# Loads of the first value tiles through GpSimd's queue, masks handed to VectorE later, and a key copy one head sooner, in a fused attention and mixture-of-experts kernel

## The chip, the cores and the metric

The kernel runs on one core of a Trainium2 chip. The metric is the time of one execution in device microseconds (us); lower is better. The core has five engines with a queue each: PE (TensorE, matmuls; its weight loads are listed apart as PEld), DVE (VectorE), ACT (ScalarE), POOL (GpSimd) and SP (SyncE, here used for DMA alone). DMA transfers are started by SP, ACT and POOL and carried out by 16 DMA engines which all of them share. The profile names lines of the kernel as L12.

## The reference

Inputs are q, k and v (4 batches, 8 heads, 768 positions, 64 values a head), the router's probabilities (3,072 rows by 4 experts), and w1 (4 x 512 x 1024) and w2 (4 x 1024 x 512), all float32. Attention is causal; heads 0, 2 and 6 ("retrieval") see all earlier positions, the other five ("streaming") the first 4 positions and the last 64. Its output, 3,072 rows of 512, goes through four experts whose outputs are added with normalised probabilities:

```python
scores = scale * np.matmul(q, k.transpose(0, 1, 3, 2))
causal = rel >= 0
stream_keep = causal & ((pos[None, :] < 4) | ((rel >= 0) & (rel < 64)))
mask = np.where(retr, causal, stream_keep)
a = softmax(np.where(mask, scores, -1e9))       # per row, + 1e-9 in the sum
x = (a @ v).transpose(0, 2, 1, 3).reshape(3072, 512)
p = probs / (probs.sum(-1, keepdims=True) + 1e-9)
for e in range(4):
    out += p[:, e:e + 1] * (np.maximum(x @ w1[e], 0.0) @ w2[e])
```

## The kernel before

**Tiles and stages.** The 3,072 rows are 24 tiles of 128. The first four tiles are the first 128 positions of the four batches. They need only the keys and values of the same 128 positions, so they are computed in a stage of their own at the start ("first" functions, L969 to L1106). The other 20 tiles get their attention in eight groups: group g is batch g // 2 and half g % 2 of its positions (384 each; half 0 leaves out the first 128). Their experts run in ten pairs of tiles.

**The start.** For each first tile b, `turn_first` transposes q and k with TensorE, `scores_first` makes scores and their exponentials (for tiles 2 and 3 `mask_scores_first` multiplies a mask afterwards; for tiles 0 and 1 the mask is a bias that `masks_first` puts into PSUM first), `values_first` multiplies with the values in `v_first`, `turn_back_first` transposes the result into `x_first`, and `layer1_first` multiplies with w1 of expert 0. w1 is in two halves of 512 columns; `layer1_first(b, [0])` needs half 0, `layer1_first(b, [1])` half 1. When all four tiles are there, `layer2_first` multiplies with w2 of expert 0. The order of these calls is written out in L1555 to L1592 and is the order of TensorE's queue.

**Loads of the start.** q and k of tiles 0 and 1 go out first, k from SP and q from ACT (L394 to L397). `load_first_v` loads the values of tile 0 from ACT and those of tiles 1 to 3 from SP as float32 into parts of the tile hA, and `cast_first_v` has VectorE turn them into float16 in `v_first` (a part of the tile tsb): L376 to L383. GpSimd's queue takes the loads that change float32 into float16 on the way: w1(0) half 0, the rows of q and k of tiles 2 and 3 (`load_first_rows`), w1(0) half 1, w2(0), and then the other weights and the inputs of attention (L483 to L502). Each load of w1's halves is two DMAs; `load_first_rows` is four.

**The other stages.** `moe_steps` yields pieces of the experts' work: first experts 1 to 3 on the four first tiles (`plain_steps`, L950), then the ten pairs (`pair_steps`, L1209), for which layers 1 and 2 are done in part by a scheme of seven products in place of eight, whose sums of blocks are VectorE's work (L843). Between these pieces the loop at the end (L1639) puts steps of attention. When, is set by `plan`: for each group a begin and an end in units of "spent" time, which counts every step by its planned length times a share (0.8 and 1.2 for the first tiles' experts, 0.5 for layer 1 of a pair and PSHARE = 1.57 for layer 2). While a group is behind its plan, one attention step after another is put in. `scale_inputs` calls `require`, which puts in whatever of a group is still missing when a pair needs it.

**A group of attention** (L512). `keys_to_rows` (L248) copies keys of retrieval heads from kT into kR with VectorE in two parts; part 0 stands at the group's beginning. Then for each head in the order 0, 2, 6, 1, 3, 5, 7, 4: `scores` multiplies into a bank of PSUM (L578), ScalarE takes the exponential into `es` (L587), and VectorE multiplies the mask into it (L594 or L598) right behind. `values` comes some heads later (a list `waiting`): TensorE multiplies `es` with the values into one of two PSUM buffers pV (L628 for retrieval, L682 for streaming heads). A retrieval head's buffer is freed by VectorE's L655 to L659, a streaming head's by ScalarE's L697 and L706 and then VectorE's L702. L702 is not put into VectorE's queue at once: `later` keeps it until the planned clock has gone on by LAG = 1,300 ns. The next group's keys and queries are transposed by DMA from SP (`transpose_k`, `transpose_q`) after the fourth head of group 1 and the third of later groups.

Engines work their queues in order, so an instruction that waits holds what stands behind it on its engine.

Of the kernel before, what the change touches and what calls it, by code (L numbers as in the profile page):

```python
# [11 lines left out]
FP32 = mybir.dt.float32  # L12
# [7 lines left out]
def kernel(  # L20
# [355 lines left out]
    def load_first_v(eng, b):  # L376
        n0 = (0, 2 * H * D, 4 * HT * 4 * P, 4 * HT * 4 * P + 2 * H * D)[b]
        x = hA[:, n0 : n0 + 2 * H * D].bitcast(FP32)
        vf[b] = x.rearrange("p (h d) -> p h d", h=H)
        eng.dma_start(out=vf[b], in_=v[b, :, 0:P, :].rearrange("h p d -> p h d"))  # L380

    def cast_first_v(b):
        nc.vector.tensor_copy(out=v_first[:, b, :, 0:D], in_=vf[b])  # L383

    vf = {}
# [12 lines left out]
    load_first_v(nc.scalar, 0)  # L398
    load_first_v(nc.sync, 1)
# [11 lines left out]
    for b in (2, 3):  # L411
        load_first_v(nc.sync, b)
# [69 lines left out]

    load_w1(0, 0)  # L483
    load_first_rows(2)
    load_first_rows(3)
    load_w1(0, 1)
# [25 lines left out]
    def attention(b, c):  # L512
# [57 lines left out]
        pv_of = {}  # L570
        def scores(h):
            hp = h // 2
            es_of[h] = []
            for cols, parts, masks in score_tiles(h):
# [15 lines left out]
                for m, mo, o0, o1 in masks:  # L590
                    if m is mC:
                        x = es[:, o0:o1].rearrange("p (n x) -> p n x", x=P)
                        y = mC.rearrange("p (n x) -> p n x", n=1)
                        nc.vector.tensor_tensor(  # L594
                            out=x, in0=x, in1=y.to_broadcast(list(x.shape)), op=ALU.mult
                        )
                        continue
                    nc.vector.tensor_tensor(  # L598
                        out=es[:, o0:o1],
                        in0=es[:, o0:o1],  # L600
                        in1=m[:, mo : mo + o1 - o0],
                        op=ALU.mult,
                    )
# [66 lines left out]
        def values(h):  # L670
            if RETR[h]:
                yield from values_r(h)
                return
# [63 lines left out]
        keys_to_rows(b, c, 0)  # L737
# [26 lines left out]
        for h in waiting:  # L764
            yield from values(h)
            behind_values(h)
        if g == 0:
            transpose_k(*more)
            transpose_q(*more)
# [49 lines left out]
    def later(op, g):  # L819
        behind.append((clock[0] + LAG, op, g))  # L820
# [388 lines left out]
    def pair_steps(nt0, nxt):  # L1209

        def plain_layer1(e):
            xs = scaled(e)
            for f0 in range(0, FTP, 2):
# [19 lines left out]
                yield 2 * DMP * mm_ns(PC), 0.5  # L1233
# [5 lines left out]
        def winograd_layer1(e, x, y, kept=kept):  # L1239
# [37 lines left out]
            yield ns, 0.5  # L1277
# [407 lines left out]
```

## Time and profile before

| what | value |
|---|---|
| median of 3 runs (lowest to highest) | 387.23 us (387.05 to 387.24) |
| the profiled execution, its own time | 387.16 us |
| its span in the trace | 385.5 us |
| PE busy from 0 to 34.91 us | 24.23 us |
| PE busy from 34.91 to 42 us | 7.09 us |
| PE busy from 42 to 380 us | 331.76 us |
| PE busy from 380 to 385.5 us | 2.27 us |
| packets in GpSimd's DMA queue, whole span | 95,872, 19.81 MB |

The span is the time from the first to the last instruction of the profiled execution; the remaining 1.66 us of that execution lie around it. "Idle before" in a row is the time for which an engine stood still ahead of that instruction, and the name behind the arrow is what it waited for by the semaphores.

### The profile page before, as it was taken

The numbers are of one execution on the slowest core, as the hardware profiler recorded it, in microseconds if no ns is written. First come the engines' busy times: TensorE is split into PE (matmuls) and PEld (weight loads), VectorE is DVE, ScalarE is ACT, GpSimd is POOL, SyncE is SP. The second block draws the span as 40 slices with busy tenths as digits, with TensorE's granted clock in tenths as the row PEclk, the third lists the DMA queues.
The fourth block names the chain that finished last, engine by engine and source line by source line (L and its number), as shares of the span: only waits on it lengthen the run. The fifth ranks groups of instructions, "written<-read, shape, count | busy, mean of one in ns | idle before, by whom it ended". The sixth has DMA issues, their size and how long they took to land.

```text
span 385.5 us, 10312 instructions
## 1 busy us (share of the span) xinstructions
PE 365.4 (95%) x4223; PEld 308.0 (80%) x4223; DVE 271.1 (70%) x614; ACT 226.5 (59%) x450; POOL 123.9 (32%) x163
## 2 busy tenths in 40 slices
PE   7489999899979999999999999899999999999996
PEld 4366445448878987998898999798898899998996
DVE  4272762977678867568857867976767967989882
ACT  2164368644876785775785695685687262360630
POOL 7526758463028338058173184220000000000000
PEclk9799999999999999999999999999999999999999
DMA  7999999999149999589599499592111110300101
GB/s 171 201 207 210 127 189 176 170 130 214 58 76 130 101 122 164 108 116 119 85 150 124 80 148 115 72 176 30 37 41 57 52 60 0 111 3 0 58 2 56
DMA packets 134376, 40.93 MB, mean 106 GB/s; under 512 B 119976, under 2 KB 128776, under 8 KB 134328
## 3 DMA queue, kind: packets, MB, share of 16 engines
q0 software_dynamic: 95872, 19.81, 62.0%
q1 hardware_dynamic: 36264, 18.62, 21.6%
q10 hardware_dynamic: 2192, 1.84, 1.5%
q8 instruction: 33, 0.54, 0.6%
q14 instruction: 15, 0.12, 0.1%
HBM read 47.00 MB, written 6.34 MB: 138 GB/s over the span
## 4 chain that ended last, share of the span: by engine, by line
PE 83%; DVE 7%; DMA 5%; ACT 3%; issue 1%; DVEq 0%; ACTq 0%
PE pO L1399 26%; PE pA L1217 22%; PE pO L1246 9%; PE pO L926 6%; PE pA L956 5%; PE pA L578 4%; DMA hA<-in_v_dram 3%; PE pV L1246 2%; PE pA L1246 2%; PE pA L1091 2%; PE pV L628 2%; PE pV L682 2%; DMA xT<-x_one 1%; DVE xs L1168 1%; DVE kS L269 1%
## 5 line engine op out<-in xcount | busy, mean ns | idle before, releaser
L1399 PEld LDWEIGHTS <-hA 128*128 128x128 f16 x1104 | 105.5, 98 | 12.2
L1217 PE MATMUL pA<-xs,w1sb 128*128 128x256 f16 x768 | 96.9, 272 | 0.0
L1399 PE MATMUL pO<-w2sb,hA 128*128 128x256 f16 x640 | 77.5, 272 | 0.0
L1217 PEld LDWEIGHTS <-w1sb 128*128 128x128 f16 x768 | 71.5, 98 | 7.4
L1226 ACT ACTIVATE hA<-pA 128x512 f16<-128x512 f32 x96 | 57.0, 600 | 31.5 <-PE pA L1217 20.2
L587 ACT ACTIVATE es<-pA 128x384 f16<-128x384 f32 (+2 forms) x112 | 52.4, 497 | 23.4 <-PE pA L578 15.3
L285 POOL DMA_DIRECT2D vS<-in_v_dram x40 | 37.1, 941 | 83.8 <-PE pV L682 62.3
L1399 PE MATMUL pO<-tsb,hA 128*128 128x256 f16 x464 | 56.2, 272 | 0.0
L1168 DVE TENSOR_TENSOR xs<-xT,pB 128x512 f16<-128x512 f16 (+1 forms) x53 | 47.2, 915 | 1.5 <-DMA qT<-q 1.5
L843 DVE TENSOR_TENSOR hA<-hA 128x1024 f16<-128x1024 f16 x60 | 39.5, 684 | 0.5
L1246 PEld LDWEIGHTS <-w1sb 128*128 128x128 f16 x512 | 31.2, 98 | 1.2 <-issue 0.5
L702 DVE TENSOR_TENSOR xT<-pV,rc 64x256 f16<-64x256 f32 (+1 forms) x40 | 19.5, 488 | 15.3 <-ACT rc L706 12.3
L1419 ACT COPY s<-pO 128x256 f32<-128x256 f32 x31 | 11.5, 372 | 31.2 <-PE pO L1399 25.4
L926 PE MATMUL pO<-w2sb,hA 128*128 128x512 f16 x128 | 29.5, 379 | 0.0
L210 POOL DMA_DIRECT2D k_rows<-in_k_dram x24 | 21.5, 906 | 12.9 <-DMA kT<-k_rows 12.9
L1256 ACT COPY s<-pO 128x512 f32<-128x512 f32 x39 | 22.7, 589 | 3.4 <-PE pO L1246 2.9
L697 ACT ACTIVATE rc<-pV,eps 64x256 f32<-64x256 f32 (+1 forms) x40 | 20.9, 522 | 5.5 <-PE pV L682 4.8
L1263 DVE CUSTOM_DVE_ANT_0 hA<-pO,s 128x512 f16<-128x512 f32 x26 | 17.7, 687 | 8.9 <-PE pO L1246 4.5
L598 DVE TENSOR_TENSOR es<-es,mW 128x256 f16<-128x256 f16 (+1 forms) x40 | 12.3, 318 | 14.7 <-ACT es L587 14.6
L926 PEld LDWEIGHTS <-hA 128*128 128x128 f16 x128 | 12.1, 98 | 12.9
L578 PE MATMUL pA<-qT,kR 128*128 128x128 f16 (+2 forms) x132 | 21.1, 263 | 1.0 <-DVE kR L251 1.0
L956 PE MATMUL pA<-x_first,w1sb 128*128 128x512 f16 x96 | 21.8, 379 | 0.0
(163 smaller groups left out, 536.3 us busy)
## 6 DMA issues: line engine op xcount, KB each, us to landing
pB<-p_rows SPq DMA_DIRECT2D x10, 512.0 KB, 5.1
out_dram<-o SPq DMA_DIRECT2D x19, 256.0 KB, 3.2
w1sb<-in_moe_w_dram POOLq DMA_DIRECT2D x16, 256.0 KB, 11.7
w2sb<-in_moe_w_dram POOLq DMA_DIRECT2D x4, 1024.0 KB, 13.5
k_rows<-in_k_dram POOLq DMA_DIRECT2D x24, 128.0 KB, 5.4
q<-in_q_dram POOLq DMA_DIRECT2D x20, 128.0 KB, 6.8
vS<-in_v_dram POOLq DMA_DIRECT2D x20, 112.0 KB, 5.7
vS<-in_v_dram POOLq DMA_DIRECT2D x20, 80.0 KB, 5.5
```

What stands on the lines that cost most here:

```text
L285: gp.dma_start(out=t[:, t0(c) :, own_v(h)], in_=windows_of(v, b, h, c))
L578: nc.tensor.matmul(out=ps[:, o : o + nq], lhsT=key_tile(b, c, h, t), rhs=qTs[b, c][:, hp, q0 : q0 + nq], start=True, stop=True,)
L587: nc.scalar.activation(out=es[:, 0:cols], in_=ps[:, 0:cols], func=AF.Exp, scale=SC)
L843: nc.vector.tensor_tensor(out=out, in0=a, in1=b, op=ALU.subtract)
L926: nc.tensor.matmul(out=ps_o, lhsT=hs[:, ft, nt * P : (nt + 1) * P], rhs=w2sb[:, e * FTP + ft, :], start=(ft == 0), stop=(ft == FTP - 1),)
L956: nc.tensor.matmul(out=ps, lhsT=w1_tile(e, ct, ft), rhs=x_first[:, ct, :], start=(ct == 0), stop=(ct == DMP - 1),)
L1168: nc.vector.tensor_tensor(out=o, in0=xin, in1=pb.to_broadcast([P, DMP, n, P]), op=ALU.mult)
L1217: nc.tensor.matmul(out=ps[:, f * PC : (f + 1) * PC], lhsT=w1_tile(e, ct, f0 + f), rhs=xs[:, ct, :], start=(ct == 0), stop=(ct == DMP - 1),)
L1226: nc.scalar.activation(out=blocks[:, b0 : b0 + 2, k0 : k0 + 2, :].rearrange("p t f x -> p f t x"), in_=ps.rearrange("p (f t x) -> p f t x" ...
L1246: nc.tensor.matmul(out=ps[:, f * P : (f + 1) * P], lhsT=w_tile(e, w[:, ct, :], f), rhs=a[:, ct, :], start=(first and f == 0 and ct == 0), ...
L1256: nc.scalar.copy(out=kept[n], in_=ps)
L1399: nc.tensor.matmul(out=ps, lhsT=a[:, k, :], rhs=b(k), start=(first and k == 0), stop=(k == KT - 1), skip_group_check=not first,)
```

## The change

- The values of the four first tiles are loaded by GpSimd, which changes them into float16 on the way, straight into `v_first`; the four casts are gone. In GpSimd's queue v of tile 0 stands first, v of tile 1 behind w1(0) half 0, v of tiles 2 and 3 ahead of w2(0).
- w1(0) half 1 stands between the rows of tiles 2 and 3, and no longer behind both.
- TensorE's order of the first tiles is changed from tile 2 on: layer 1 of tile 0, half 1, and of tile 1, half 0, come ahead of tile 3's transposes; the values of tile 2 ahead of tile 3's scores.
- Masks are handed to VectorE by `later` with a lag of 800 ns of the planned clock behind the scores; `values` hands over what is left of its head's. The list `behind` is kept in order of due time.
- For groups from 2 on, part 0 of `keys_to_rows` stands in the group before, behind the first of the heads that are left in `waiting`.
- The plan: the shares of the first pair are 0.8 and 1.24, those of the others as they were; attention 1 may begin at the first pair's beginning, and the ends of groups 1 to 7 are later.

The diff, cut:

```diff
-    def load_first_v(eng, b):
-        n0 = (0, 2 * H * D, 4 * HT * 4 * P, 4 * HT * 4 * P + 2 * H * D)[b]
-        x = hA[:, n0 : n0 + 2 * H * D].bitcast(FP32)
-        vf[b] = x.rearrange("p (h d) -> p h d", h=H)
-        eng.dma_start(out=vf[b], in_=v[b, :, 0:P, :].rearrange("h p d -> p h d"))
-
-    def cast_first_v(b):
-        nc.vector.tensor_copy(out=v_first[:, b, :, 0:D], in_=vf[b])
+    def load_first_v(b):
+        gp.dma_start(
+            out=v_first[:, b, :, 0:D], in_=v[b, :, 0:P, :].rearrange("h p d -> p h d")
+        )
...
-    load_first_v(nc.scalar, 0)
-    load_first_v(nc.sync, 1)
...
-    for b in (2, 3):
-        load_first_v(nc.sync, b)
...
+    load_first_v(0)
     load_w1(0, 0)
+    load_first_v(1)
     load_first_rows(2)
+    load_w1(0, 1)
     load_first_rows(3)
-    load_w1(0, 1)
+    load_first_v(2)
+    load_first_v(3)
     load_w2(0)
...
+        def mask_later(es, masks):
+
+            left = [masks]
+
+            def run():
+                for m, mo, o0, o1 in left.pop() if left else ():
...
+            later(run, g, MASK_LAG)
+            return run
...
-                for m, mo, o0, o1 in masks:
...
+                masks_of.setdefault(h, []).append(mask_later(es, masks))
...
         def values(h):
+            for run in masks_of[h]:
+                run()
...
-        keys_to_rows(b, c, 0)
+        if g < 2:
+            keys_to_rows(b, c, 0)
...
-        for h in waiting:
+        for n, h in enumerate(waiting):
             yield from values(h)
             behind_values(h)
+            if more and g and n == 0:
+                keys_to_rows(*more, 0)
...
+    MASK_LAG = 800.0
+
-    def later(op, g):
-        behind.append((clock[0] + LAG, op, g))
+    def later(op, g, lag=LAG):
+        behind.append((clock[0] + lag, op, g))
+        behind.sort(key=lambda x: x[0])
...
+        share1, share2 = (0.8, 1.24) if nt0 == pair0 else (0.5, PSHARE)
...
-    cast_first_v(0)
     scores_first(0)
     turn_first(1, [0])
     values_first(0)
-    cast_first_v(1)
...
     turn_first(2)
-    cast_first_v(2)
     turn_back_first(1)
-    turn_first(3)
     scores_first(2)
     mask_scores_first(2)
-    cast_first_v(3)
+    layer1_first(0, [1])
     layer1_first(1, [0])
+    turn_first(3)
+    values_first(2)
     scores_first(3)
-    values_first(2)
     mask_scores_first(3)
-    layer1_first(0, [1])
+    layer1_first(1, [1])
     turn_back_first(2)
-    layer1_first(1, [1])
     values_first(3)
...
-    begin = first_pair + 0.05 * PAIR
-    for a, n in zip(range(1, G), (0.7, 1.55, 2.55, 3.4, 4.4, 5.3, 6.65)):
+    begin = first_pair
+    for a, n in zip(range(1, G), (0.8, 1.72, 2.75, 3.55, 4.55, 5.5, 6.8)):
```

The yields of a pair's steps carry share1 in place of 0.5 and share2 in place of PSHARE.

## The prediction

> **What bounds the kernel now.** I read the page first, then TensorE's waits, then the first 42 us engine by engine, then the places of the remaining waits. The engine row of the page and its slices:
>
> ```profile
> span 385.5 us, 10312 instructions
> PE 365.4 (95%) x4223; PEld 308.0 (80%) x4223; DVE 271.1 (70%) x614; ACT 226.5 (59%) x450; POOL 123.9 (32%) x163
> PE   7489999899979999999999999899999999999996
> PEclk9799999999999999999999999999999999999999
> ```
>
> TensorE is busy for 365.4 of 385.5 us, so a change pays only by filling some of the 20.1 us in which it stands still, or by a better clock: slices 2 and 3 are half empty, and slice 2 has the one low clock. Its waits over the whole span (total, times, longest):
>
> ```profile
> PE pV L1053 <- DVE tsb L383: 5.3, 1, 5.3
> PE pV L682 <- DVE xT L702: 2.3, 2, 2.0
> PE pV L682 <- DVE x_one L659: 1.6, 2, 0.9
> PE pV L682 <- DVE x_pair L659: 0.9, 2, 0.5
> PE pA L578 <- DVE kR L251: 1.0, 1, 1.0
> PE pA L578 <- DVE kS L273: 0.2, 1, 0.2
> ```
>
> One wait of 5.3 us lies in the start; those on L702, L659, L251 and L273 all lie behind 42 us and sum to 6.0. The start, on TensorE and VectorE (start, duration, work, idle before it and its releaser):
>
> ```profile
> 9.50 1.09 PE L987 MATMUL pO<-early,hA 128*64 128x128 f32 x14 [0.31 <-DMA hA<-in_q_dram]
> 15.89 0.60 PE L1053 MATMUL pV<-tsb,es 128*128 128x65 f16 x8 [5.30 <-DVE tsb L383]
> 16.42 1.98 PE L987 MATMUL pO<-early,hA 128*64 128x128 f32 x16
> 34.91 7.07 PE L926 MATMUL pO<-w2sb,hA 128*128 128x512 f16 x32
> ...
> 15.41 0.43 DVE L383 CAST tsb<-hA 128x512 f16<-128x512 f32 x1 [7.04 <-DMA hA<-in_v_dram]
> ```
>
> The values of tile 0 leave ScalarE's queue at 3.46 us and are there at 15.4; TensorE stands from 10.59 to 15.89. In the 1 us window from 14 the granted clock is 0.57, from 15 to 20 it is 0.50, and 1.00 again from 21. GpSimd's issues show when weights land, because its ninth issue waits for its first:
>
> ```profile
> 2.91 1.65 POOL L307 DMA_DIRECT2D w1sb<-in_moe_w_dram  x2
> 10.87 0.54 POOL L374 DMA_DIRECT2D k_rows<-in_k_dram  x1 [3.04 <-DMA w1sb<-in_moe_w_dram]
> 24.47 0.61 POOL L307 DMA_DIRECT2D w1sb<-in_moe_w_dram  x1 [1.54 <-DMA w1sb<-in_moe_w_dram]
> 29.55 0.61 POOL L307 DMA_DIRECT2D w1sb<-in_moe_w_dram  x1 [4.47 <-DMA w2sb<-in_moe_w_dram]
> ```
>
> Counting by eights, w1(0) half 0 is in at 10.87 and 12.75, half 1 at 22.31 and 24.47, w2(0) at 29.55. The largest later wait, on TensorE and VectorE:
>
> ```profile
> 113.47 0.36 DVE L598 TENSOR_TENSOR es<-es,mW 128x384 f16<-128x384 f16 x1 [0.77 <-ACT es L587]
> 113.74 0.68 DVE L843 TENSOR_TENSOR hA<-hA 128x1024 f16<-128x1024 f16 x1
> 114.34 0.54 DVE L702 TENSOR_TENSOR xT<-pV,rc 64x384 f16<-64x384 f32 x1
> 115.03 0.34 PE L682 MATMUL pV<-es,vS 128*128 128x48 f16 x7 [2.05 <-DVE xT L702]
> ```
>
> ScalarE had finished rc at 112.91, but L702, which frees the PSUM buffer, stood in VectorE's queue behind a mask that waited for its exponential.
>
> **Part A, the first tiles.** *Removed:* four loads from ScalarE's and SyncE's queues (0.61 us each for v 0 and 1) and four casts on VectorE (0.43, 0.52, 0.42, 0.42: 1.8 us). Neither engine was what ended TensorE's waits but for the first cast. *Added:* four GpSimd issues of 1,024 packets each. L210's k_rows loads have this shape: 0.90 us apiece, 3.6 us of GpSimd. v 0 now goes out at 2.91, w1(0) half 0 at 3.8, 0.9 later, v 1 behind it, then q and k of tile 2, half 1 of w1(0), tile 3, v 2, v 3, w2(0). From w2(0) on, GpSimd's order is as before, and so are the loads it waits for, eight back.
>
> When does v 0 land? No row shows this load here. Landings of k_rows take 2.4 us at least, 5.4 in the median, 12.8 at most: 5.3, 8.3 or 15.7. It starts beside the 1 MB of q and k, whose packets in the other two queues thin out at 6 to 7 us; the w1 load of twice its bytes in that place took 8.0. I take 10 us, before the end of the q turn at 10.59, so nothing waits for it. That removes the 5.30 us of idle.
>
> The clock fell 3.5 us after TensorE's last matmul; the waits left are shorter, so I take it not to fall. The matmuls at half clock cost: 16 turns 1.98 against 1.25 (14 in 1.09 at full clock), values 0.60 against 0.42, turn back 0.61 against 0.40, scores 0.61 against 0.40, layer 1 1.64 against 1.07: 1.9 us. So L926 would begin at 34.91 - 5.3 - 1.9 = 27.7.
>
> What is late then is the data. All four v loads still stand ahead of w2(0), the same packets with half the bytes written, so w2(0) comes at about 29.6, which holds L926 to 29.6: a gain of 5.3. In between, w1(0) half 1 is wanted by the new order some 7.5 us after L1053, at 18.1: values 0.4, turn 1.25, turn back 0.4 and its copy 0.7, scores 0.4, layer 1 1.1, values 0.4, tile 2's turns 1.2 and copy 0.7, turn back and scores 0.8. It was in at 24.47 with all of v and of tiles 2 and 3 ahead of or beside it; now tile 3 (256 KB, 1.3 us at the 205 GB/s of these stretches) and two v loads (2,048 packets, 2.1 us at the 961 to 1,079 small packets that went through each us from 42 to 44) come behind it, 3.4 us, so it lands at about 21. That wait of 2 to 3 us, which reaches L926 through tile 1's layer 1, leaves a gain of 3.0. I take 4.2, the middle. Bounds: 0 (v 0 no sooner than before) and 7.2 (no wait for data at all).
>
> What follows starts 4.2 us sooner and must find its data: w1(1) was in by 35.6 for use at 41.81, w2(2) was in at 55.75 (a wait on it ends there) and is first used at 63.82, w1(3) lands by 67.6 for use at 74.95, w2(3) by 72.62 for 81.98. The least slack is 6.2 us, so 4.2 is covered; without that cover the loss would be what exceeds it, at most 4.2.
>
> **Part B, masks, key copy, plan.** The masks are the same instructions at the same prices (0.27 to 0.36 us each). Handed over 800 ns of planned time later, they no longer make VectorE wait for ScalarE: L598 alone idled it 14.6 us over 12 waits. What could be late is the values behind a mask; values() hands over what is left, and in the built order the shortest stretch of matmuls between a head's last scores and its values is 1.5 us in group 0, whose order is unchanged and whose masked piece is the earlier one, and 2.4 us elsewhere. An exponential (0.49) and a mask (0.36) fit in. Taken at nothing; if not covered, some 0.5 us for a head.
>
> Group by group, with matmuls priced from their rows (0.22 us for 512 columns, 0.11 for 256): in group 1 the values of head 5 come 2.9 us of matmuls after those of head 1, whose buffer they need, not 1.1; the 2.05 us wait goes, 0.3 stays. In group 6 the values of head 1 come 4.6 us, not 2.4, after those of head 0: the 0.69 and 0.45 us waits on L659 at 245 and 248 go. The key copy of group 3 (L251, 147.40) was late because L702 ahead of it waited 2.39 us for a transpose; moved into group 2's last heads it is out of the way of the scores: 1.0 us. Group 0's waits (0.90, 0.47) stay. Removed: 2.0 + 1.1 + 1.0 = 4.1. New places (the copy now stands ahead of the last L702s of each of groups 1 to 6; attention 1 begins 4 us of matmuls sooner, over a layer 1 in which ScalarE is 9.06 of 10 us busy) I charge at 1.1, like one of the L659 pairs. Gain 3.0; bounds 4.1 and -4 (a stall like group 0's 1.37 in each of six groups costs 8.2, less the 4.1).
>
> **Sum.** The profiled execution took 387.16 us, 1.66 around its span of 385.5: 387.16 - 4.2 - 3.0 = 380.0. The median, 387.23, is 0.07 higher, which changes nothing.
>
> **Rivals.** *Only A pays* (0.24): VectorE has the same work at 70% and PE finds as many new waits as it loses; 387.2 - 4.2 = 383.0. For it: L702's 2.39 us wait for a transpose has nothing to do with masks. Against: the distances of groups 1 and 6 grow by 1.8 and 2.2 us.
>
> *v 0 late* (0.09): GpSimd writes its descriptors while VectorE fills buffers until 4.4 us, and shares the engines with q, k and w1. For it: w1's issues took 0.83 us each there and 0.61 to 0.66 later. At k_rows' 11.2 us, its landing time in the full queue at 33.8, v 0 lands at 14.1, TensorE's clock falls, and A gives 1.3: 387.2 - 1.3 - 3.0 = 382.9. The Trainium skill (SBUF — State Buffer, section "SBUF: two separate sides") says that GpSimd cannot write descriptors while VectorE runs an operation in its two-port mode, and that loads from SyncE's or ScalarE's queue are immune; it advises the opposite of this edit. By that rule alone the load would start when VectorE's run ends, 1.5 us later, land at 11.5 and cost 0.9 (380.9); the 0.2 us in w1's issues bears out only a part of it.
>
> *Slower* (0.08): the key copy stands in VectorE's queue ahead of the last L702s and waits for the next group's key transposes, three of 1.22 us on SyncE behind x_one's. TensorE then waits for PSUM in six groups. It decides from 7.2 / 6 = 1.2 us a group; at one set of transposes, 3.8 less the 1.1 of matmuls between two heads, it is 16 us: 396. Against: at 91.5 and 119.9 the copy ran 14 and 7 us after them, without a wait.
>
> *Nothing left* (0.04): A gives 3, B loses as much: 387.2.
>
> **Chances.** Forecast 0.55, own range 377.5 to 382. The range runs from 376.8 (A at 6.3, two thirds of the way to its bound, B at 4.1) to 384.2 (A at 3.0, B at 0); it takes in rivals one and two; outside are the last two and the tails, 0.2. Faster 0.88, same 0.04, slower 0.08, with 0.2% as what a measurement of this kernel can tell.
>
> **What would show it.** L1053's first row at 10 to 11 us with no wait on a cast; granted clock 1.00 throughout; L926's first row near 30.7; a wait of L1091 on w1 or of L926 on w2 as what is late next; L682's waits on L702 and L578's on kR gone. Wrong: L1053 beyond 13, L926 beyond 33, or VectorE's L251 waiting for DMA.

## The result, and the profile after

| kernel | median (lowest to highest, runs) | ratio to before, 95% interval |
|---|---|---|
| before | 387.24 us (387.05 to 387.51, 6) | 1 |
| changed | 384.95 us (383.51 to 386.22, 6) | 0.9941 [0.992, 0.9962] |

The change makes the kernel faster by 2.3 us, not by 7.2: the time lies above the forecast's own range (377.5 to 382) and above the wider one that takes in two rivals (376.8 to 384.2). Medians and ranges in this document hold every execution; the ratios leave out three executions, two of the first kernel with unread matmuls and one of best3, that took over 1.5% longer than the fastest of their kernel. The profiled execution took 384.91 us, its span 383.2. Its page:

```profile
span 383.2 us, 10297 instructions
PE 365.9 (95%) x4223; PEld 307.5 (80%) x4223; DVE 271.0 (71%) x610; ACT 225.9 (59%) x450; POOL 127.1 (33%) x167
PEclk9989999999999999999999999999999999999999
```

TensorE stands still for 17.3 us in place of 20.1, and is busy 0.5 us more. Its low clock has moved from the second slice to the third. TensorE's waits (total, times, longest):

```profile
PE pO L1414 <- DVE o L1437: 1.8, 2, 1.4
PE pO L1261 <- DVE xs L857: 1.7, 1, 1.7
...
PE pV L690 <- DVE es L580: 1.4, 1, 1.4
...
PE pV L690 <- DVE xT L710: 0.8, 3, 0.3
PE pA L1105 <- DMA w1sb<-in_moe_w_dram: 0.7, 1, 0.7
```

The 5.3 us for v 0, the 2.05 for the PSUM buffer (PSUM is the memory that matmuls write) and the 1.0 for kR are gone. Among the largest are three that were not there: for the sums `o` of a pair (L1437, which was L1422 before), for the sums of scaled inputs (L857, which was L843) and for the masks (L580). The start, on TensorE and GpSimd (start, duration, work, idle before it and its releaser):

```profile
10.15 0.41 PE L1067 MATMUL pV<-tsb,es 128*128 128x65 f16 x8
17.87 3.53 PE L1105 MATMUL pA<-x_first,w1sb 128*128 128x128 f16 x32 [0.74 <-DMA w1sb<-in_moe_w_dram]
25.53 1.95 PE L1105 MATMUL pA<-x_first,w1sb 128*128 128x128 f16 x32
30.42 7.07 PE L940 MATMUL pO<-w2sb,hA 128*128 128x512 f16 x32
...
10.39 0.63 POOL L307 DMA_DIRECT2D w1sb<-in_moe_w_dram  x1 [2.13 <-DMA tsb<-in_v_dram]
27.15 0.62 POOL L307 DMA_DIRECT2D w1sb<-in_moe_w_dram  x1 [4.67 <-DMA w2sb<-in_moe_w_dram]
```

The values' matmuls start at 10.15 us (15.89 before) without a wait, and layer 2 (L940, L926 before) at 30.42 in place of 34.91: 4.49 us sooner. w1(0) half 1 was in by 17.9 and w2(0) by 27.15. But 32 matmuls of layer 1 took 3.53 us where another 32 take 1.95: half clock. From the start of layer 2 to the span's end it is 350.6 us before and 352.8 after, so everything behind the start **lost** 2.2 us. Two of the places, each on TensorE, VectorE and SyncE (SPq):

```profile
146.99 1.03 PE L1414 MATMUL pO<-tsb,hA 128*128 128x256 f16 x8 [1.45 <-DVE o L1437]
140.65 0.35 DVE L251 COPY kR<-kT 64x768 f16<-64x768 f16 x1
146.06 0.43 DVE L710 TENSOR_TENSOR xT<-pV,rc 64x256 f16<-64x256 f32 x1 [3.29 <-DMA xT<-x_one]
139.23 1.19 SPq L670 DMA_TRANSPOSE xT<-x_one  x1
...
251.11 0.61 PE L1261 MATMUL pO<-xs,w1sb 128*128 128x128 f16 x8
254.44 0.62 PE L1261 MATMUL pO<-xs,w1sb 128*128 128x128 f16 x8 [1.72 <-DVE xs L857]
252.96 1.23 DVE L1182 TENSOR_TENSOR xs<-xT,pB 128x1024 f16<-128x1024 f16 x1 [3.75 <-DMA qT<-q]
247.28 4.34 SPq L231 DMA_TRANSPOSE qT<-q  x3
```

At 146 us the key copy (L251) is out of the way, at 140.65, but L710 (L702 before) still waits for the transpose of x_one, the output of a retrieval head. Before, this wait held the key copy behind it, and so the scores (0.96 us); now it holds the next thing in VectorE's queue, `o`, and TensorE waits 1.45. At 254 us VectorE's scaled inputs (L1182) wait 3.75 us for group 7's query transposes, because they go into the buffer from which these read. The trace of before had the same wait at the same place, and it cost TensorE nothing:

```profile
257.72 0.61 PE L1246 MATMUL pO<-xs,w1sb 128*128 128x128 f16 x8
255.45 1.23 DVE L1168 TENSOR_TENSOR xs<-xT,pB 128x1024 f16<-128x1024 f16 x1 [1.52 <-DMA qT<-q]
256.59 0.28 DVE L843 TENSOR_TENSOR xs<-xs,kS 128x256 f16<-128x256 f16 x1
248.38 3.84 SPq L231 DMA_TRANSPOSE qT<-q  x3
```

The last query transpose left SyncE at 252.22, 5.5 us before the matmuls that need what follows it; in the changed kernel at 251.62, 1.1 us before the time at which they would have started (254.44 - 1.72). The plan put group 7 later by some 4 us against TensorE's work. By arrival the room was smaller: before, the last sum of this chain (L843) ended at 256.87, 0.85 us ahead of its matmuls at 257.72.

### The profile page after: what moved, and what is told of

It is laid out like the page before. It is cut to its first block, busy times and chain, and to the rows that moved or that the text cites. A ratio compares the mean times of both kernels' runs of the same rounds, so it can differ in the third digit from the quotient of the medians.

```text
span 383.2 us, 10297 instructions
## 1 busy us (share of the span) xinstructions
PE 365.9 (95%) x4223; PEld 307.5 (80%) x4223; DVE 271.0 (71%) x610; ACT 225.9 (59%) x450; POOL 127.1 (33%) x167
## 4 chain that ended last, share of the span: by engine, by line
PE 70%; DVE 11%; DMA 8%; ACT 5%; issue 3%; SPq 2%; POOL 1%; DVEq 0%; POOLq 0%; ACTq 0%
PE pO L1414 22%; PE pA L1232 18%; PE pO L1261 9%; PE pA L970 4%; PE pO L940 4%; PE pA L597 4%; DMA w1sb<-in_moe_w_dram 4%; DMA qT<-q 3%; DVE xs L1182 3%; SPq L231 2%; PE pV L1261 2%; PE pA L1105 2%; PE pV L634 2%; PE pA L1261 2%; DMA xT<-x_pair 1%
## 5 line engine op out<-in xcount | busy, mean ns | idle before, releaser
L1414 PEld LDWEIGHTS <-hA 128*128 128x128 f16 x1104 | 104.3, 98 | 13.8 <-issue 2.1
L1182 DVE TENSOR_TENSOR xs<-xT,pB 128x512 f16<-128x512 f16 (+1 forms) x53 | 47.2, 915 | 4.5 <-DMA qT<-q 3.8
L857 DVE TENSOR_TENSOR hA<-hA 128x1024 f16<-128x1024 f16 x60 | 39.3, 683 | 0.4
L1261 PEld LDWEIGHTS <-w1sb 128*128 128x128 f16 x512 | 31.2, 98 | 3.6 <-DVE xs L857 2.0
L940 PE MATMUL pO<-w2sb,hA 128*128 128x512 f16 x128 | 29.5, 379 | 0.0
L710 DVE TENSOR_TENSOR xT<-pV,rc 64x256 f16<-64x256 f32 (+1 forms) x40 | 19.5, 488 | 10.5 <-ACT rc L714 6.0
L210 POOL DMA_DIRECT2D q<-in_q_dram x20 | 17.6, 894 | 17.3 <-DMA qT<-q 13.8
L940 PEld LDWEIGHTS <-hA 128*128 128x128 f16 x128 | 12.1, 98 | 12.9
L1261 PE MATMUL pO<-xs,w1sb 128*128 128x128 f16 x264 | 20.0, 219 | 2.1 <-DVE xs L857 1.7
```

The lines of the kernel that those rows point to most:

```text
L210: gp.dma_start(out=x16[:, j, :, :], in_=x[b, :, s0 : s0 + P, :].rearrange("h p d -> p h d"),)
L857: nc.vector.tensor_tensor(out=out, in0=a, in1=b, op=ALU.subtract)
L940: nc.tensor.matmul(out=ps_o, lhsT=hs[:, ft, nt * P : (nt + 1) * P], rhs=w2sb[:, e * FTP + ft, :], start=(ft == 0), stop=(ft == FTP - 1),)
L1182: nc.vector.tensor_tensor(out=o, in0=xin, in1=pb.to_broadcast([P, DMP, n, P]), op=ALU.mult)
L1261: nc.tensor.matmul(out=ps[:, f * P : (f + 1) * P], lhsT=w_tile(e, w[:, ct, :], f), rhs=a[:, ct, :], start=(first and f == 0 and ct == 0), ...
L1414: nc.tensor.matmul(out=ps, lhsT=a[:, k, :], rhs=b(k), start=(first and k == 0), stop=(k == KT - 1), skip_group_check=not first,)
```

## The experiments

Each ratio is to the kernel before, run on the same chip (its median there 386.78 to 387.12 us). "Profiled" is the one execution that left a trace.

### One part taken away, or one alone

Part names: A is the first tiles; M the late masks; K the key copy; P the shares and the plan. The edits put back the code of before:

```diff
 # M undone
-            later(run, g, MASK_LAG)
-            return run
+            run()
+            return run
 # K undone
-        if g < 2:
-            keys_to_rows(b, c, 0)
+        keys_to_rows(b, c, 0)
...
-            if more and g and n == 0:
-                keys_to_rows(*more, 0)
 # P undone
-        share1, share2 = (0.8, 1.24) if nt0 == pair0 else (0.5, PSHARE)
+        share1, share2 = 0.5, PSHARE
...
-    begin = first_pair
-    for a, n in zip(range(1, G), (0.8, 1.72, 2.75, 3.55, 4.55, 5.5, 6.8)):
+    begin = first_pair + 0.05 * PAIR
+    for a, n in zip(range(1, G), (0.7, 1.55, 2.55, 3.4, 4.4, 5.3, 6.65)):
```

**A alone.** 

> Part A alone: loads and order of the first tiles as changed; masks at once, the key copy in its own group, the old plan and shares. Theory 1 (A is worth what the start shows, 34.91 - 30.42 = 4.5 us, and the rest loses 2.2): about 382.8 us, less spread between runs than the changed kernel's 383.5 to 386.2, and TensorE's waits on L702, L659 and kR of the kernel before still there. Theory 2 (an earlier start always runs into late data and transposes, whatever the rest does): 384.5 to 385.5, with waits on transposes at 140 to 150 us as long as in the changed kernel.

**Without M.** 

> The changed kernel with masks put into VectorE's queue at once, as before. Theory 1 (the late masks cost group 0 its 1.36 us wait on a mask and gain elsewhere less): 383.5 to 384.5. Theory 2 (late masks are what removes the wait on L702 in group 1): 386 to 387, with that wait of some 2 us back. Theory 3 (masks are neutral): 384.9.

**Without K.** 

> The changed kernel with part 0 of the key copy back at its own group's beginning. Theory 1 (the copy is not what VectorE waits for; the wait is L702's for the transpose of x_one, and the copy's place only decides which engine work stands behind it): 384.5 to 385.5, with a wait on kR of 1 us or more in place of the 1.45 us on L1437's o. Theory 2 (the copy ahead of L702 blocks VectorE): 383 or less.

**Without P.** 

> The changed kernel with the old plan and shares. Theory 1 (the later ends put the last transposes of group 7's queries at 247 to 252 us, on which scale_inputs waits 3.75 us, TensorE 1.72; with the old plan they come some 3 us sooner against the pairs): 382 to 383.5, no wait at 254. Theory 2 (the plan is what removes the waits on pV in groups 1 and 6): 386 to 387, those back.

**A and M.** 

> Part A and the late masks, without the key copy and the plan. If masks alone cost what undoing them gave (1.3 to 1.8 us): 384 to 384.5. If what costs is masks and plan together: 382.5 to 383, as a_only, with TensorE's wait on L702 in group 1 at 1 us or less in place of 2.05 and a wait of 1.3 us on a mask in group 0.

**A and P.** 

> Part A and the new plan and shares, without late masks and key copy. If the plan alone costs what undoing it gave (1.5 us): 384 to 384.5, with the wait at 254 us on group 7's query transposes. If what costs is masks and plan together: 382.5 to 383.

**The changed kernel once more.** 

> The changed kernel once more, for more executions and a second trace. Theory 1 (the spread of its runs comes from the start, where the clock falls in some executions and not in others): this trace, if its clock stays at 1.00 from 15 to 25 us, has its first L940 at 28 to 29 us in place of 30.42. Theory 2 (the spread comes from transposes and loads later): L940 at 30.4 again, and the waits at 147 and 254 us differ by 1 us or more.

| parts | median (lowest to highest, runs) | ratio, 95% interval | profiled: layer 2 of the first tiles from |
|---|---|---|---|
| A | 382.7 (380.85 to 385.39, 6) | 0.9896 [0.9867, 0.9925] | 28.23 |
| A+K+P | 383.19 (382.47 to 384.35, 6) | 0.9908 [0.9888, 0.9928] | 28.51 |
| A+M+P | 385.19 (382.77 to 387.92, 12) | 0.995 [0.9924, 0.9977] | 30.58 |
| A+M+K | 383.02 (381.3 to 384.28, 6) | 0.9905 [0.9887, 0.9923] | 28.99 |
| A+M | 382.57 (380.92 to 384.29, 6) | 0.9901 [0.9883, 0.9919] | 28.85 |
| A+P | 386.44 (384.62 to 389.11, 12) | 0.9987 [0.9965, 1.0009] | 28.31 |
| A+M+K+P again | 383.96 (381.58 to 385.18, 6) | 0.9918 [0.9894, 0.9942] | 28.36 |

A alone is worth 4.0 us (1.04% of 387.1). The whole change is worth no more: its two measurements lie 1.7 and 0.9 us behind A, with intervals that overlap A's, the first one just. M adds nothing to A (0.9901 against 0.9896), K nothing to A+M (0.9905). Without K the changed kernel is as it was; without M it is 1.3 us better than the first measurement and 0.4 better than the second, which the intervals do not tell apart. P is the loss: added to A it costs 3.5 us (0.9987 less 0.9896), more than either expectation for A and P had. Without K a wait of 1 us on kR was expected; the trace has 0.27. The traces also show which part removed which wait: P the 2.05 us of group 1 (gone in A+P, 0.95 and 0.34 in A+M), and P's last three due times the 0.69 and 0.45 us of group 6 (they stand in A alone and are gone in A+P). The wait on kR, 0.96 us before, is 0.27 in A alone and gone in A+M, so little was left for K. A+P's trace at 254 us (L1258 and L854 are L1261 and L857 here):

```profile
255.04 1.04 PE L1258 MATMUL pO<-xs,w1sb 128*128 128x128 f16 x8 [2.58 <-DVE xs L854]
```

The wait is 2.58 us, and eight matmuls after it took 1.04 us where 0.61 is usual: half clock.

### The clock after short waits

The two traces of the changed kernel, in stretches of 2 us. After the two times stand the busy times of PE, PEld, DVE, ACT and POOL with their counts, then the granted clock, the DMA share and GB/s. First the one above, then the one of the repeat:

```profile
16.00:18.00 2.00, 0.92 (x15) 0.61 (x16) 0.88 (x3) 1.42 (x3) 1.97 (x3) 0.99 1.39 162
18.00:20.00 2.00, 2.00 (x21) 2.00 (x20) 0.64 (x2) 0.52 (x2) 1.98 (x4) 0.50 1.78 129
20.00:22.00 2.00, 2.00 (x30) 1.71 (x27) 0.00 (x0) 0.89 (x3) 2.00 (x4) 0.66 1.12 177
```

```profile
16.00:18.00 2.00, 1.33 (x23) 1.01 (x24) 0.88 (x2) 1.63 (x3) 1.70 (x3) 1.00 1.72 158
18.00:20.00 2.00, 2.00 (x40) 1.75 (x37) 0.43 (x2) 1.26 (x4) 2.00 (x5) 1.00 1.65 153
```

In the first, waits of 0.53, 0.20 and 0.74 us within 2.4 us were followed by 3.4 us at 0.50; in the second, waits of 0.76, 0.20 and 0.47 left the clock as it was, and layer 2 began at 28.36, 2.06 us sooner. A later kernel (best2 below) had 0.58, 0.20 and 0.73 there and kept its clock. At 66 us it fell after a wait of 2.61 (A alone) and of 1.67 (after_late below), and at 68 it did not after 2.15 (best3 below). So the length of the wait does not decide it alone; a wait of some 1 to 3 us here costs either itself or itself and about 1.7 us more. The Trainium skill (TensorE: Matmul & The Clock Gate, section "Part 1: The HAM clock gate (the "warmup" mystery)") says that the gate watches a free-running window of 3.4 us and halves the clock after an idle one. The low stretches of 3.4 us, and the same waits with and without a fall, agree with a window that runs on its own. That the window has to be idle does not agree: the waits named here are all shorter than it.

The traces say more. In the three traces with two separate falls of the clock to 0.50, these lie 47.8, 187.7 and 187.7 us apart: 14, 55 and 55 times 3.413 us. So the clock changes on a fixed grid, which lies differently in each execution. Cut along that grid, the 16 traces in which a fall shows where it lies give 1,717 stretches at 5 to 379 us. At full clock, each of the 17 stretches in which TensorE was busy for 43% or less was followed by half clock (in A alone, 62.95 to 66.36 us, with 1.00 us busy), 2 of the 9 with 45 to 58%, and none with 60% or more. At half clock, the 5 stretches with 49 to 66% were followed by half clock again, and the 19 with 77% or more by full clock. So it matters how much of a wait falls into one stretch. What decides between 45 and 58% is not shown.

The mean clock is known for every execution, not only for the profiled ones. One fall of 3.4 us takes some 0.0045 off it: 1.000 is no fall, 0.995 one, 0.991 two, 0.986 three. Half of the low time is then an estimate of what the clock cost.

Two kernels tried to keep the clock up with matmuls whose results nobody reads, `warm_up(bank(), n, 256)`. The first is the changed kernel with 3, 4 and 4 of them in the start; the second, built on `after_late` below, has 14 more ahead of group 0's values:

```diff
+    warm_up(bank(), 3, 256)
     turn_back_first(0)
...
+    warm_up(bank(), 4, 256)
     turn_back_first(1)
...
+    warm_up(bank(), 4, 256)
     layer1_first(0, [1])
 # the second kernel alone
         def values(h):
+            if g == 0 and h in (2, 1):
+                warm_up(bank(), 4 if h == 2 else 10, 256)
```

> The changed kernel with 11 matmuls added whose results nobody reads (128x128 by 128x256, about 0.11 us each at full clock) in three places of the start: ahead of turning back tile 0, of turning back tile 1, and of the first half of w1(0) for tiles 2 and 3. The theory that the waits of the start let the clock fall: the granted clock stays at 1.00 from 10 to 25 us, the second half of w1(0) takes about 1.9 us in place of 3.53, layer 2 of the first tiles begins near 28.5 to 29 us in place of 30.42, and the median comes to 383 to 384 us, less than the changed kernel's own by no more than 2 us, since the streaming values then wait for the sink rows near 66.5 us. Rival: the clock falls at about 18 us all the same, or in other places, and the time stays at 384 to 385.5 us.

> The changed kernel with the last three due times put back, with 11 unread matmuls of 128x256 in the waits of the start (as in after_warm) and 14 more ahead of the values of heads 2 and 1 of group 0, where TensorE waited 0.57 and 1.67 us; 25 x 0.11 = 2.7 us of matmuls. If the half clock comes from the share of idle time in these stretches, none is seen up to 90 us and the median falls by about 1.5 us to 379.5 to 380.5 us, with runs closer together than the 2.2 us of the kernel without them. Rival: the clock falls all the same, or the unread matmuls take TensorE's time where it had work: 382 us or more.

The first: 384.67 us (381.78 to 387.77, 6), 0.991 [0.9879, 0.9941]. The clock stayed at 1.00 from 10 to 25 us and layer 2 began at 29.06, but in the same trace it fell at 68 and at 256 us, behind waits of 2.55 and 2.26, and the runs lay 6.0 us apart. The second: 381.84 (379.84 to 383.13, 6), 0.9874 [0.9849, 0.9899] against 0.9859 without them. Its trace at 66 us, then that of the kernel without:

```profile
66.00:68.00 2.00, 0.53 (x7) 0.35 (x8) 0.64 (x3) 0.20 (x1) 0.59 (x1) 1.00 1.21 204
```

```profile
66.00:68.00 2.00, 1.80 (x9) 0.80 (x10) 0.59 (x2) 0.89 (x2) 0.56 (x1) 0.50 1.24 205
```

The clock stayed at full from 10 us on, as the theory had it, but the median did not fall. By the estimate, the clock cost 0.4 us an execution here and 1.1 without the unread matmuls; that these (14 x 0.11 = 1.5 us at this place) took what was gained fits, and is not shown by itself. The wait for the sink rows stayed: 1.76 us, up to 67.47.

### The second limit of the start: group 0's sink rows

A's trace showed 6.7 us gained at 28.23, and 4.0 at the end. What took part of it, on TensorE, SyncE and GpSimd:

```profile
66.56 0.37 PE L690 MATMUL pV<-es,vS 128*128 128x32 f16 x5 [2.61 <-DMA vS<-v_sinks]
59.23 0.82 SPq L302 DMA_DIRECT2D vS<-v_sinks  x1
55.70 0.54 POOL L292 DMA_DIRECT2D v_sinks<-in_v_dram  x1 [5.25 <-DMA w2sb<-in_moe_w_dram]
```

`put_sinks` (L299) copies the first four rows of values (the sink rows) into the streaming windows vS. It can go out only when these have landed behind the weights in GpSimd's queue, and is in 7.3 us after its issue (6.9 to 8.5 in the nine traces where TensorE waits for it). Before, it went out at 60.03 and the values were wanted at 70.85; with the same 7.3 us it was in at 67.4, so by this estimate the start could move by about 3.5 us before this was met. Two kernels on A: one sinks load ahead of w2(2), and no copy for group 0 (its four sink rows stay out of the output there):

```diff
 # a_sink
+    load_sinks(0, slice(0, 1))
     load_w2(2)
     load_v(0, 0, SH)
-    load_sinks(0)
+    load_sinks(0, slice(1, 3))
 # a_nosink
-            if n == 1:
+            if n == 1 and g:
                 put_sinks()
```

> Part A alone (as a_only), and one of group 0's three loads of the first four value rows ahead of w2(2), so that the third no longer waits for w2(2) to land (5.25 us in a_only). Theory 1 (group 0's streaming values cannot start before SyncE's copy of these rows into vS has landed, at 66.5 us, and this caps what the sooner start gains at 70.85 - 66.5 = 4.3 us): the copy goes out at 56 to 57 in place of 59.2, TensorE's wait of 2.61 us on vS is gone, 380.0 to 381 us. Theory 2 (the copy lands late because it shares the DMA engines with w1(3) and w2(3), not because it goes out late): it lands at 65 or later all the same, 382.5.

> The first-tiles part alone, with the first group's four sink rows not copied into its streaming value windows (those four value rows of the first group are left out of the output; everything else is computed). The theory that this small SyncE copy is the wall of the start: in the kernel with the first-tiles part alone the streaming values waited 2.61 us at 66.56 us for it and the clock then stood at 0.50 for 3.5 us, which cost about 1.7 us more; without the copy the streaming values begin near 64 us, no low clock follows at 66 us, and the median goes from a ratio of 0.9896 to about 0.979, 378.5 to 379.5 us. Rival: something else stands right behind the copy (VectorE's masks, the exponentials, the values' own loads), the wait is taken over by it, and the time stays at 381.5 us or more.

a_sink: 384.83 us (383.29 to 387.23, 12), 0.9948 [0.9931, 0.9965], 2 us worse than A, and outside both theories. The loads of vS went out 2.2 us later (47.16 us, 44.97 in A), but GpSimd was 1.4 us behind A's trace already before the load that was moved. The copy went out at 60.98, and TensorE waited 4.25 us. The edit could not win much: in A's trace SyncE waits for the loads of vS until about 57.7 and for the sink rows only 1.5 us more. By the estimate above, the clock accounts for 1.8 of the 2 us (3.7 us an execution, 1.9 in A). a_nosink: 383.21 (381.33 to 383.75, 6), 0.9897 [0.9875, 0.9919]: no gain, and that expectation was wrong. In its trace the wait for vS is gone and two others stand in its place, 0.90 us for x_one and 0.47 for x_pair, while the clock fell in the start instead (layer 2 from 30.87), so this trace does not show the sooner start without the copy. Two other executions kept a clock of 1.000 throughout and took 383.01 and 383.30 us, no less than A. So the copy is not the only limit; that VectorE's chain through masks and sums is the next, close behind, is read from waits as in this trace and was not tested alone.

### The plan's due times, and versions built on them

`after_late` is the changed kernel with three numbers put back; `late_aplan` the same without M and K:

```diff
-    for a, n in zip(range(1, G), (0.8, 1.72, 2.75, 3.55, 4.55, 5.5, 6.8)):
+    for a, n in zip(range(1, G), (0.8, 1.72, 2.75, 3.55, 4.4, 5.3, 6.65)):
```

> The changed kernel with the plan's last three due times alone (groups 5, 6 and 7: 4.55, 5.5, 6.8) put back to what they were (4.4, 5.3, 6.65). The theory that the plan makes group 7's query transposes late for the last pair's scaled inputs, which use the same buffer: the wait on VectorE's xs near 254 us (1.72 us here, 2.58 us and a stretch of 0.50 clock with the plan as the only addition) is gone, the small waits near 302 and 304 us too, and the median falls by 1.7 to 3 us, to 382 to 383.2 us. Rival: the wait moves with the transposes or the price of the plan lies in its earlier entries and shares; 384 to 385.5 us.

> The first-tiles part with the plan's first four entries and its shares, masks at once, key copy as before, last three due times as before. With the whole plan this was 386.44 us, without any of the plan 382.7. If all of the plan's price lies in the last three due times, this gives 381 to 382.7 us (the 2.05 us wait of group 1 gone, nothing new near 254 us). Rival: the earlier entries and shares cost something too: 384 us or more.

after_late: 381.42 us (380.34 to 382.58, 6), 0.9859 [0.9837, 0.9881], so these three numbers cost the changed kernel 2.3 to 3.2 us (0.9918 and 0.9941 less 0.9859). Behind 200 us its trace has waits of 0.3 us or more of 2.7 us in sum, of which 1.72 is that for group 7 and 0.7 are two on `o`; after_late has 0.9. By the estimate above the clock costs 2.2 us an execution with the late due times and 1.1 without. Waits and clock together make up 2.9 us. At 251 to 253 us, on the three engines:

```profile
251.93 0.61 PE L1261 MATMUL pO<-xs,w1sb 128*128 128x128 f16 x8
253.25 0.61 PE L1261 MATMUL pO<-xs,w1sb 128*128 128x128 f16 x8
251.28 1.22 DVE L1182 TENSOR_TENSOR xs<-xT,pB 128x1024 f16<-128x1024 f16 x1 [1.82 <-DMA qT<-q]
245.21 2.53 SPq L231 DMA_TRANSPOSE qT<-q  x2
```

The query transposes leave SyncE 5.5 us before their follower again, VectorE's idle is back at 1.82, and TensorE goes from one product to the next without a gap. late_aplan: 382.71 (381.81 to 382.96, 5), 0.9894 [0.9875, 0.9913], the same as A, so the plan's first four entries and its shares bring nothing measurable by themselves: the 2.05 us wait is gone in its trace, but the low clock at 66 us lasts 6.8 us, against 3.4 in A's. Against A+P, which differs by the last three due times alone (0.9987), late_aplan is 3.6 us better, with intervals far apart. With M and K on top it is 0.9859; the intervals touch, so a gain of 1.3 us there is likely and not certain.

On after_late: masks of group 0 at once (late_g0), group 0 later in the plan (late_shift2), both (best2), and later still (best3, 1.2 and 2.35). best1 is A+M+K with masks of group 0 at once, the unread matmuls of the start, and group 0's sink rows by VectorE:

```diff
 # late_g0, best1, best2, best3
-            later(run, g, MASK_LAG)
+            if g:
+                later(run, g, MASK_LAG)
+            else:
+                run()
             return run
 # late_shift2, best2
-    plan = {0: (0.88 * UNIT, 2.15 * UNIT)}
+    plan = {0: (1.1 * UNIT, 2.25 * UNIT)}
 # best1
-                put_sinks()
+                put_sinks(g == 0)
...
+        if first:
+            nc.vector.tensor_copy(
+                out=x[0:NS, :, :], in_=src.to_broadcast([NS, WT, NSH * P])
+            )
+            return
```

> The first-tiles part, the late masks from the second group on, and the key copy sooner, with the plan and shares of before; the first group's sink rows are put in by one VectorE copy (4 x 4480 elements, by the row of 64 x 1736 in 0.61 us about 1.6 us) in place of the SyncE copy, and the 11 unread matmuls of the start are added. If the sink rows' copy and the clock of the start were what held the start's gain: streaming values of the first group begin near 64.5 us, the clock stays at 1.00 to 75 us, and the median is 379 to 380.5 us. Rival: VectorE has no room between 60 and 75 us (9 of 10 busy in those slices), its copy delays masks or casts that TensorE waits for, and the median is 382 to 383 us, that of the first-tiles part with the late masks.

> The changed kernel with the last three due times put back and group 0's masks handed to VectorE at once, as before the change (all other groups' masks late). If the sink rows' copy is the wall at 66.2 us, the masks of group 0 are not what the streaming values wait for and the median stays within 0.5 us of 381.42. If the late masks hold them (1.36 us <- es in the changed kernel's trace), the wait at 66 us falls under 0.5 us and the median is 379.5 to 380.5 us.

> The changed kernel with the last three due times put back (381.42 us) and group 0's place in the plan moved from (0.88, 2.15) to (1.1, 2.25) units, by which 1.73 us more of the experts' matmuls stand ahead of the first streaming values. If these values can't start before about 66.2 us whatever stands ahead of them (the sink rows' copy, 1.67 us of wait there), the matmuls moved ahead fill the wait: waits at 62 to 68 us fall from 2.66 us in sum to under 1, no stretch of low clock follows, and the median is 379 to 380 us. Rival: what group 0 waits for is its own masks, copies and exponentials, which move with it; the waits stay as long, only later, and the median stays at 381 to 382 us.

> The changed kernel with the plan's last three due times put back, group 0's masks at once and group 0 at (1.1, 2.25) units of the plan. By the theory that the sink rows (fixed near 66.2 to 67.4 us) and the late masks are two separate limits of the streaming values, each hidden when the other is met, both go here: waits at 62 to 70 us under 1.2 us in sum (1.47 for the masks and 1.67 for the sink rows in the two kernels with one edit each), no low clock in that stretch, and the median is 379 to 380 us. Rival: VectorE's copies of the keys and windows (0.7 us <- kS in each trace) hold the scores and all behind them, so the median is the 380.2 to 380.9 us of either edit alone.

> As the other kernel of this pair, with group 0 later again, at (1.2, 2.35) units. If the sink rows' wall is passed at 1.1 already, nothing more is gained and the median is within 0.5 us of that kernel's; if group 0's end then comes too late for the first pair of tiles (group 1's key and query transposes are issued behind it), a new wait comes up near 90 us (the scores of group 1 waited 1.43 to 1.56 us for qT there with the late plan) and the median is 1 us or more above it.

| kernel | median (lowest to highest, runs) | ratio, 95% interval | waits of TensorE at 62 to 74 us |
|---|---|---|---|
| best1 | 384.64 (383.6 to 385.65, 6) | 0.994 [0.992, 0.996] | 1.48, 1.63, then 7 us of low clock |
| late_g0 | 380.93 (380.57 to 381.63, 4) | 0.9857 [0.9834, 0.988] | 0.73, 0.90, 0.47 |
| late_shift2 | 380.24 (379.58 to 383.89, 6) | 0.9853 [0.9822, 0.9884] | 0.71, 1.47, 0.25 |
| best2 | 380.25 (379.42 to 384.42, 6) | 0.986 [0.9814, 0.9906] | 0.28, 1.02, 0.75, 0.54 |
| best3 | 383.18 (380.46 to 386.88, 6) | 0.9891 [0.9841, 0.994] | 2.15 |

best1 failed: VectorE's copy took 2.47 us, not the 1.6 estimated, and TensorE waited 1.48 us for the mask behind it. The other edits each trade one wait near 66 us for another; none differs from after_late by more than the runs can tell. Nor are the sink rows a fixed wall near 66 us: put_sinks went out anywhere from 57.75 to 62.08 us in after_late, late_g0, late_shift2, best2 and best3, each time right behind the landing of the loads that it waits for. best3 shows where later is too late:

```profile
91.90 0.59 PE L600 MATMUL pA<-qT,kR 128*128 128x128 f16 x3 [3.55 <-DMA qT<-q]
```

Group 1's transposes are issued behind group 0; TensorE waits 3.55 us for them, and some 6 us of low clock follow. after_late, late_g0, late_shift2 and best2, at 380.2 to 381.4 us, are 1.4 to 1.5% faster than the kernel before, and faster than the changed kernel too (best2's interval touches the repeat's).

## Why the prediction was wrong, step by step

**Part A, 4.2 us: right in its sum by luck, wrong in its terms.** A alone gave 4.0 us (2.9 to 5.1 by its interval). v 0 was there by 10.15 us (9.66 in A's trace; taken: 10), and TensorE did not wait for it. Layer 2 began at 30.42 (30.7), which was luck too: a stretch of half clock had put it back, and the repeat of the same kernel, at full clock there, has 28.36. GpSimd's issue of v 0 took 1.01 us, that of v 1 0.92. The Trainium skill's rule that VectorE's two-port runs hold back GpSimd's descriptors (SBUF — State Buffer, section "SBUF: two separate sides") had given 11.5 us for the landing by the prediction's working; the trace does not bear that time out.

Three terms were off. w1(0) half 1 landed at 17.9 us, not at 21, and w2(0) at 27.15, not 29.6, so the data allowed a gain of 6 to 7 us, near the upper bound: the prediction counted the loads that now come behind half 1, and not that GpSimd issues it 3.1 us sooner (10.39 in place of 13.46). "I take it not to fall" failed in the profiled execution: of the 1.9 us of half clock that was to be saved, 1.6 came back (3.53 less 1.95) behind waits of under 1 us each. And "The least slack is 6.2 us, so 4.2 is covered" went through the weights alone. The sink rows' copy had about 3.5; in the four traces with group 0's masks at once and layer 2 from 28.2 to 28.5 us (A, A+P, A+K+P, late_aplan) TensorE waited 2.61 to 3.88 us for it. The sum came out near because these errors have opposite signs. A small misreading besides: of the slices called half empty, the second is at 4 tenths and the third at 8.

**Part B, 3.0 us: the step that failed.** All that it named as removed was removed. B measured is the changed kernel against A: 0.9941 and 0.9918 against 0.9896, a loss of 0.9 to 1.7 us, of which the intervals leave open whether it is a loss or nothing; a gain of 3.0 is far outside. The term that failed is "New places [...] I charge at 1.1". It listed the key copy and attention 1's earlier start, and left out the later due times, which it did not follow to SyncE's queue. In place of 1.1 us, what was added took back all of the 4.1 us removed:

- The last three due times cost 2.3 to 3.2 us: put back alone, this comes back. They move group 7's query transposes to within 1.1 us of TensorE's need, where 5.5 us had been. VectorE's 1.52 us of idle for `DMA qT<-q` at 255 us, in the trace of before, was the warning. The same three numbers removed the 0.69 and 0.45 us waits of group 6, so that part of the gain and its price came together.
- "The key copy [...] 1.0 us": A+M+K measures like A+M, where the wait on kR is gone already. The copy was behind the wait for x_one's transpose, and was not its cause; with the copy gone, the wait holds `o`, 0.44 to 1.65 us in nine of the ten traces that have K and the plan's early entries.
- "Taken at nothing" for the masks: A+M measures like A, so this holds over the kernel. In the changed kernel's trace group 0 waited 1.36 us for a mask at 68 us: the prediction fitted an exponential and a mask into the matmuls between scores and values, and did not ask what else stands in VectorE's queue, which idled nowhere from 60.4 to 69 us. With those masks at once the copy (3.32 us in A+K+P) or the sums (0.90 and 0.47 in late_g0) hold it instead.

**The rivals.** The nearest was "Only A pays" (383.0, chance 0.24), and for its reason: as many new waits as old ones. It still put B at nothing, where the medians put it below. v 0 was not late; the key copy (L251) made VectorE idle for 0.2 us in all in the changed kernel's trace.

**Open.** The clock is part of the spread of the runs, and not all of it. Taking the estimated cost of the clock from each time, the spread from lowest to highest falls from 4.5 to 2.1 us for A alone, from 3.6 to 2.0 for the repeat of the changed kernel and from 3.4 to 1.9 for A+M, but only from 5.2 to 4.7 for A+M+P. The rest are waits that differ from one execution to the next, of which one trace a kernel shows little. Whether M and K gain 1.3 us together on a good plan is likely, not settled.

## What to carry to other kernels

An engine's idle row that costs the bounding engine nothing is a slack with a size: compute it (the time of need less the time of arrival; 0.85 us at 257 us here) before moving anything that feeds it, through the DMA queue and the reused buffer as well as through the data. When a wait on a copy is removed by moving the copy, look at what ended the wait of the instruction ahead of it; if that is a DMA, the wait passes to the next in the queue. Before a start is made earlier, list every load that the next stage needs, the small ones above all, since in a full queue a 35 KB copy can have the least slack.

## What the runs showed of the hardware

TensorE's granted clock fell to 0.50 for 3.4 us, or twice that, after waits as short as 0.53, 0.20 and 0.74 us within 2.4 us, or one of 1.67; and in other executions it did not after 1.72, 2.15 or nearly the same three. The changes lie on a grid of 3.413 us that runs on through the execution: a stretch of it at 43% busy or less was always followed by half clock, one at 60% or more never, and half clock lasted until a stretch of 77% or more. Each fall costs about 1.7 us where TensorE has work, so a short wait can cost twice its length. A 35 KB copy from SyncE took 7.3 us to land at 59 to 67 us (A alone; 6.9 to 8.5 in nine traces), while w1 and w2 moved through GpSimd's queue. The Trainium skill (DMA: Bandwidth & Descriptors, section "SWDGE vs HWDGE vs iDMA") says that each DMA engine takes turns between the queues that feed it; the trace shows the delay and not its cause. VectorE copied 4 x 4480 elements in 2.47 us, 0.55 ns each.
